# A retention-and-FFN kernel: k and q of two pairs loaded and transposed together, v behind them

## The chip, the cores and the metric

The kernel runs on one core of a Trainium2 chip. The metric is the device time of one launch in microseconds: 224.27 us is the median of 3 runs of the kernel before (224.18 to 224.47). The profile is of one execution with a span of 224.2 us; the granted TensorE clock is full speed (1.0) throughout.

## The reference

Two stages follow each other. The first is a decayed linear attention with a recurrent state, for 4 batches, 8 heads, 768 tokens and head size 64; the second is a gated feed-forward layer over all 3072 tokens, with 512 features and 1536 hidden columns.

```python
gamma = 1.0 - 2.0 ** (-5.0 - np.arange(H))
for t in range(S):
    state = gamma[None, :, None, None] * state + np.einsum('bhd,bhe->bhde', k[:, :, t], v[:, :, t])
    y[:, :, t] = scale * np.einsum('bhd,bhde->bhe', q[:, :, t], state)

x = y.transpose(0, 2, 1, 3).reshape(B * S, H * D)
gate = 1.0 / (1.0 + np.exp(-(x @ w_gate)))
out = (gate * (x @ w_val)) @ w_out
```

All inputs and the output are float32 in HBM; the kernel computes in bfloat16 with float32 sums.

## The kernel before, in words

**Tiles.** The 768 tokens are cut into six chunks t of 128. A chunk of all four batches (512 rows) is one unit of the feed-forward stage. The attention works on "pairs": pair i = 2t + h is chunk t of batches 2h and 2h + 1, all 8 heads. So there are twelve pairs; pairs 4 and 5 are chunk 2, pair 6 is the first half of chunk 3.

**Attention of a pair.** Its k, q and v are loaded by GpSimd with a cast to bfloat16: k and q in three DMAs each (`load_kq`, `load_swapped`, L62 to L74: one of 128 KB at L66 and two of 64 KB at L70), v in one of 256 KB (`load_v`, L57 to L60). For the scores, k and q are needed with the head dimension on the partitions. From pair 3 on this is done by two crossbar DMAs per pair, issued by SyncE (`xbar`, L216 to L220): one for k (`kqX<-kn`), one for q (`kqX<-qn`). Then:

- `quarter_scores` (matmuls of L248) needs the pair's transposed k and q
- `mask` (VectorE, L261) multiplies the scores by the decay
- `inter` (L271) multiplies transposed q by the state of the pair two before
- `intra` (L278) multiplies the masked scores by v
- `state` (L301) multiplies the scaled k (`scale_k`, GpSimd, L224) by v, and `state_sum` (L310) adds it to the state
- `y_out` (L294) writes the attention's result as the input of the feed-forward stage

`block(old, new, st)` (L316 to L336) puts these in the order that TensorE gets: inter of old, scores of new, intra of old, state of st.

**Feed-forward of a chunk.** `up` (twelve groups, matmuls of L391) computes gate and value; ScalarE takes the sigmoid (L419) and VectorE the product (L420). `down` (eight groups, L391 too) multiplies by w_out; ScalarE copies the sums out (L441) and SyncE stores them (L442). The feed-forward of chunk t runs while the attention of the next chunks is worked in between its groups.

**What sets the order.** Every engine executes its instructions in program order, and the order is written out by hand. After the first chunk, `plan` (L574 to L584) lists for every chunk t which step goes behind which of its 20 groups (0 to 11 are `up`, 12 to 19 are `down`). In the loop at L592 a step is emitted behind its group; but each step's instructions run as soon as their own engine comes to them. GpSimd has the loads, `scale_k` and `hold`, and is ahead of TensorE. SyncE has the crossbar DMAs and the output stores in one queue.

`hold` (L536 and L537) is a copy of one column of transposed data on GpSimd, whose result nobody uses. It makes GpSimd wait until that crossbar DMA has landed, so that the loads listed behind it don't run beside the transfer. By default it waits for q (`which=1`), with a second argument of 0 for k.

**Around the change.** Before the plan starts, L556 to L559 put on GpSimd `scale_k(3)`, `hold(3, 0)` and all loads of pairs 4 and 5 in the order k, q, v of 4, k, q, v of 5 (`load_next`, L530 to L532). In the plan for t = 1, `xbar(4)`, `scale_k` of 4 and 5, `hold(4)` and the loads of pair 6 stand behind group 4, and `xbar(5)` behind group 7. Pair 4's scores and its state stand behind group 11, pair 4's inter and intra with pair 5's scores and state behind group 14, and pair 5's inter and intra with pair 6's scores and state behind group 18. `xbar(6)`, `scale_k(6)`, `hold(6)` and the loads of pair 7 stand behind group 12.

GpSimd's loads use a set of eight completion semaphores in turn, so a load can't be issued before the one eight places earlier has landed. The buffers concerned are six for k and v each, four for q and four for the transposed pairs (`kqX`).

Of the kernel before, what the change touches and what calls it, by code (L numbers as in the profile page):

```python
# [9 lines left out]
BF16 = mybir.dt.bfloat16  # L10
# [5 lines left out]
def kernel(  # L16
# [16 lines left out]
    C = 128  # L33
    NT = S // C
    NP = H // 2
# [10 lines left out]
    at = ctx.enter_context(tc.tile_pool(name="at", bufs=2))  # L46
# [3 lines left out]
    kn, qn, ks, vs, kqT = {}, {}, {}, {}, {}  # L50
# [6 lines left out]
    def load_v(i):  # L57
        t, h = divmod(i, 2)
        vs[i] = ld.tile([C, 2 * H, D], BF16, tag="vs", name="vs", bufs=6)
        nc.gpsimd.dma_start(out=vs[i], in_=v[2 * h:2 * h + 2, :, t * C:(t + 1) * C, :].rearrange("b h s d -> s (b h) d"))  # L60

    def load_swapped(tiles, x, i, tag, bufs):  # L62
        t, h = divmod(i, 2)
        tiles[i] = ld.tile([C, 2 * H, D], BF16, tag=tag, name=tag, bufs=bufs)
        src = x[2 * h:2 * h + 2, :, t * C:(t + 1) * C, :].rearrange("b h s d -> b s h d")
        nc.gpsimd.dma_start(out=tiles[i][:, 0:H], in_=src[0])  # L66
        dst = tiles[i][:, H:2 * H].rearrange("s (p e) d -> s e p d", e=2)
        pairs = src[1].rearrange("s (p e) d -> s e p d", e=2)
        for e in range(2):
            nc.gpsimd.dma_start(out=dst[:, e], in_=pairs[:, 1 - e])  # L70

    def load_kq(i):
        load_swapped(kn, k, i, "kn", 6)
        load_swapped(qn, q, i, "qn", 4)  # L74
# [138 lines left out]
                nc.tensor.transpose(tp[:, which, p, :], heads(x, j, p), ident)  # L213
        nc.scalar.copy(kqT[i][:, :, j], tp)

    def xbar(i):  # L216
        kqT[i] = at.tile([128, 2, 2, NP, C], BF16, tag="kqX", name="kqX", bufs=4)
        for which, x in enumerate((kn[i], qn[i])):
            nc.sync.dma_start_transpose(out=kqT[i][:, which].rearrange("d j p s -> d (j p) s"),
                                        in_=x.rearrange("s h d -> s (h d)"))  # L220

    def scale_k(i):
        ks[i] = ld.tile([C, 2 * H, D], BF16, tag="ks", name="ks", bufs=3)
# [207 lines left out]
    def down(t, b, lo, hi, split=None):  # L431
        split = t > 0 if split is None else split
        if lo == 0:
            po[b] = bank([128, 512])
        o = po[b]
        for n1 in range(lo, hi):
            product(split, o, hT[t][:, n1, b * C:(b + 1) * C], wo[:, n1, :], start=(n1 == 0), stop=(n1 == NFF - 1))
        if hi < NFF:
            return
        ob = ffn.tile([128, D_MODEL], F32, tag="ob", name="ob", bufs=4)  # L440
        nc.scalar.copy(ob, o)  # L441
        nc.sync.dma_start(out=out[rows(t, b):rows(t, b) + C, :], in_=ob)  # L442
# [87 lines left out]
    def load_next(i):  # L530
        load_kq(i)
        load_v(i)  # L532
# [3 lines left out]
    def hold(i, which=1):  # L536
        nc.gpsimd.tensor_copy(held, kqT[i][:, which, 1, NP - 1, C - 1:C])  # L537
# [12 lines left out]
    for j in range(2):  # L550
        mask(2, j, 0)
        mask(2, j, 1)
    xbar(3)
    for b in range(3):
        down(0, b, 9, 12)
    scale_k(3)  # L556
    hold(3, 0)
    load_next(4)
    load_next(5)  # L559
    down(0, 3, 0, 6)  # L560
    new_y(2)
    inter(2)
# [2 lines left out]
    for j in range(2):  # L565
# [6 lines left out]


    plan = {  # L574
        1: [(2, block, None, 3), (4, block, 3, None, 3), (4, xbar, 4), (4, scale_k, 4), (4, scale_k, 5), (4, hold, 4),
            (4, load_next, 6), (5, casts, 3), (7, xbar, 5), (11, block, None, 4, 4), (12, xbar, 6), (12, scale_k, 6),
            (12, hold, 6), (12, load_next, 7), (14, block, 4, 5, 5), (18, block, 5, 6, 6)],
        2: [(0, xbar, 7), (0, scale_k, 7), (0, hold, 7), (0, load_next, 8), (4, casts, 4), (8, block, 6, 7, 7), (10, xbar, 8),
            (10, scale_k, 8), (10, hold, 8), (10, load_next, 9), (14, casts, 5), (17, block, 7, 8, 8)],
        3: [(2, xbar, 9), (2, scale_k, 9), (2, hold, 9), (2, load_next, 10), (4, casts, 6), (8, block, 8, 9, 9), (10, xbar, 10),  # L580
# [46 lines left out]
```

## Time and profile before

| what | value |
|---|---|
| time | 224.27 us (224.18 to 224.47) |
| TensorE busy | 215.9 us, 96% of the span |
| VectorE, ScalarE, GpSimd busy | 124.6, 70.6, 100.3 us |
| loads issued by GpSimd (queue q0) | 80960 packets, 13.90 MB, 83.8% of 16 engines' span |
| SyncE's transfers and stores (queue q1) | 23648 packets, 11.21 MB, 25.7% |
| crossbar DMA, median from issue to landing | k 6.8 us, q 4.0 us |
| load of one v, median from issue to landing | 7.3 us |
| GpSimd waiting in `hold` for transposed q | 34.6 us in 6 waits |

How to read it: the busy time of an engine is its share of the whole span, but only waits on the engine that sets the end cost anything. GpSimd's 34.6 us in `hold` are made on purpose. The chain of waits goes from the last instruction back to what released each one; the timeline shows one engine's instructions in order, with a wait in brackets behind the row that waited; the DMA issues give the time from the issue of a transfer to its landing.

### The profile page before, as it was taken

Reading aid. Unit: us, or ns where it says so; the run is one execution under the profiler, and the core shown is the slowest. Engines: PE = TensorE matmul, PEld = TensorE weight load, DVE = VectorE, ACT = ScalarE, POOL = GpSimd, SP = SyncE. Lnnn points to the kernel's source line nnn. Section 1 sums busy time; section 2 is a strip of 40 time slices with the busy share of each in tenths; the row PEclk is TensorE's granted clock in tenths of the full one; section 3 lists DMA queues with packets and bytes.
Section 4 is the critical chain, followed back from the end, with each engine's and each line's share of the span. In section 5 each row is a group of like instructions: output and inputs, shape, how many; then the busy total and the mean of one; then the engine's idle time right before and its main releaser. Section 6 shows DMA issues by size and latency. Waiting matters only on the chain.

```text
span 224.2 us, 6376 instructions
## 1 busy us (share of the span) xinstructions
PE 215.9 (96%) x2760; PEld 126.4 (56%) x2766; DVE 124.6 (56%) x252; ACT 70.6 (31%) x122; POOL 100.3 (45%) x120
## 2 busy tenths in 40 slices
PE   7789999999999997999999999999999999999994
PEld 2544444569999654556556556555555555555554
DVE  6784963194963874845925744935654922333301
ACT  4883333243233121332321332321433321333221
POOL 7999647859792935819276082550000000000000
PEclk9999999999999999999999999999999999999999
DMA  9999999999999999999979979897600012100022
GB/s 132 147 166 185 196 202 174 170 156 236 155 123 130 134 129 196 162 92 92 125 105 174 169 50 123 90 136 126 140 3 0 3 47 96 47 4 1 3 94 94
DMA packets 105820, 25.84 MB, mean 115 GB/s; under 512 B 94784, under 2 KB 102848, under 8 KB 105792
## 3 DMA queue, kind: packets, MB, share of 16 engines
q0 software_dynamic: 80960, 13.90, 83.8%
q1 hardware_dynamic: 23648, 11.21, 25.7%
q8 instruction: 21, 0.34, 0.7%
q10 hardware_dynamic: 1184, 0.33, 0.6%
q14 instruction: 7, 0.06, 0.1%
HBM read 28.31 MB, written 6.29 MB: 154 GB/s over the span
## 4 chain that ended last, share of the span: by engine, by line
PE 60%; DMA 25%; POOL 12%; issue 1%; DVE 0%; POOLq 0%; SPq 0%
PE ff L391 56%; DMA kqX<-qn 7%; DMA wo<-in_moe_w_out_dram 5%; DMA qn<-in_q_dram 4%; DMA kn<-in_k_dram 3%; DMA wv<-in_moe_w_val_dram 3%; DMA kqX<-kn 2%; PE ff L278 2%; POOL kn L70 2%; POOL vs L95 2%; POOL wg L82 2%; POOL wv L82 1%; POOL kn L95 1%; POOL kn L66 1%; POOL qn L95 1%; PE ff L248 1%
## 5 line engine op out<-in xcount | busy, mean ns | idle before, releaser
L420 DVE TENSOR_TENSOR hT<-gs,ff 128x512 bf16<-128x512 f32 x72 | 48.4, 686 | 50.3 <-PE ff L391 47.0
L391 PE MATMUL ff<-xT,wv 128*64 128x512 bf16 (+2 forms) x608 | 70.0, 345 | 0.1
L391 PE MATMUL ff<-xT,wg 128*64 128x512 bf16 (+2 forms) x606 | 69.8, 345 | 0.1
L419 ACT ACTIVATE gs<-ff 128x512 f32<-128x512 f32 x72 | 42.8, 597 | 83.2 <-PE ff L391 76.4
L391 PE MATMUL ff<-wo,hT 128*64 128x512 bf16 (+3 forms) x580 | 64.5, 361 | 0.1
L391 PEld LDWEIGHTS <-wv 128*64 128x64 bf16 (+1 forms) x608 | 35.4, 109 | 23.5
L391 PEld LDWEIGHTS <-hT 128*64 128x64 bf16 (+1 forms) x582 | 32.7, 109 | 27.1
L391 PEld LDWEIGHTS <-wg 128*64 128x64 bf16 (+1 forms) x608 | 34.9, 109 | 23.2 <-DVE xT L294 0.2
L261 DVE TENSOR_TENSOR st<-ff,maskk 128x256 bf16<-128x256 f32 (+2 forms) x76 | 35.1, 492 | 7.4 <-PE ff L248 6.4
L441 ACT COPY ob<-ff 128x512 f32<-128x512 f32 x23 | 13.5, 586 | 58.6 <-PE ff L391 58.4
L294 DVE TENSOR_TENSOR xT<-ff,taby 128x512 bf16<-128x512 f32 x20 | 12.9, 686 | 25.4 <-PE ff L278 25.4
L537 POOL COPY held<-kqX 128x1 bf16<-128x1 bf16 x7 | 1.5, 211 | 37.1 <-DMA kqX<-qn 34.6
L70 POOL DMA_DIRECT2D kn<-in_k_dram x20 | 15.1, 765 | 2.3 <-DMA kn<-in_k_dram 1.1
L70 POOL DMA_DIRECT2D qn<-in_q_dram x20 | 15.3, 790 | 1.0 <-DMA wv<-in_moe_w_val_dram 0.6
L224 POOL TENSOR_TENSOR ks<-kn,tabsk 128x1024 bf16<-128x1024 bf16 x8 | 15.6, 1956 | 0.0
L60 POOL DMA_DIRECT2D vs<-in_v_dram x10 | 12.0, 1204 | 1.1 <-DMA wo<-in_moe_w_out_dram 1.0
L66 POOL DMA_DIRECT2D kn<-in_k_dram x10 | 9.3, 926 | 2.3 <-issue 1.5
L66 POOL DMA_DIRECT2D qn<-in_q_dram x10 | 9.1, 913 | 0.8 <-DMA wv<-in_moe_w_val_dram 0.8
L314 DVE TENSOR_TENSOR zb<-za,tabz 128x512 bf16<-128x512 f32 x10 | 7.3, 734 | 0.0
L464 PE MATMUL ff<-zero 128*128 128x512 bf16 x14 | 5.6, 542 | 1.2 <-DVE zero L139 1.2
L82 POOL DMA_DIRECT2D wv<-in_moe_w_val_dram x8 | 6.7, 864 | 0.0
L82 POOL DMA_DIRECT2D wg<-in_moe_w_gate_dram x8 | 6.6, 853 | 0.0
(74 smaller groups left out, 114.4 us busy)
## 6 DMA issues: line engine op xcount, KB each, us to landing
out_dram<-ob SPq DMA_DIRECT2D x23, 256.0 KB, 2.7
vs<-in_v_dram POOLq DMA_DIRECT2D x10, 256.0 KB, 7.3
kn<-in_k_dram POOLq DMA_DIRECT2D x13, 128.0 KB, 4.8
qn<-in_q_dram POOLq DMA_DIRECT2D x13, 128.0 KB, 4.7
wo<-in_moe_w_out_dram POOLq DMA_DIRECT2D x4, 384.0 KB, 9.1
kn<-in_k_dram POOLq DMA_DIRECT2D x20, 64.0 KB, 3.7
qn<-in_q_dram POOLq DMA_DIRECT2D x20, 64.0 KB, 4.9
wg<-in_moe_w_gate_dram POOLq DMA_DIRECT2D x4, 256.0 KB, 7.5
```

What stands on the lines that cost most here:

```text
L60: nc.gpsimd.dma_start(out=vs[i], in_=v[2 * h:2 * h + 2, :, t * C:(t + 1) * C, :].rearrange("b h s d -> s (b h) d"))
L66: nc.gpsimd.dma_start(out=tiles[i][:, 0:H], in_=src[0])
L70: nc.gpsimd.dma_start(out=dst[:, e], in_=pairs[:, 1 - e])
L82: nc.gpsimd.dma_start(out=dst[:, kk, cols], in_=w.rearrange("(kk p) n -> p kk n", p=128)[:, kk, cols])
L95: eng.dma_start(out=dst, in_=x[b:b + n, :, 0:C, :].rearrange("b h s d -> s (b h) d"))
L224: nc.gpsimd.tensor_tensor(ks[i], kn[i], tabsk[:, i // 2].rearrange("s j h -> s (j h)").unsqueeze(2) .to_broadcast([C, 2 * H, D]), op=ALU.mult)
L261: nc.vector.tensor_tensor(st[i, j][to, :, n], sc[i, j][e][of, :, n], maskk[to, e ^ j, :, n], op=ALU.mult)
L294: nc.vector.tensor_tensor(xT[t][0][:, :, c:c + C], y[i, j], taby, op=ALU.mult)
L391: nc.tensor.matmul(o[c], w[:, c], x, **marks)
L419: nc.scalar.activation(g, ps[0], AX.Sigmoid)
L420: nc.vector.tensor_tensor(hT[t][:, n1s[0]:n1s[-1] + 1, lo:hi], g.rearrange("p (i n) -> p i n", n=n), ps[1].rearrange("p (i n) -> p i n", n ...
L441: nc.scalar.copy(ob, o)
```

## The change

The loads before the plan bring only k and q of pairs 4 and 5. Then the four crossbar transfers of both pairs are issued one after the other, in the order q of 5, k of 4, q of 4, k of 5. As SyncE keeps its order, the first of them waits for the load that comes last, and so all four start when all four loads have landed. `hold(5, 0)` makes GpSimd wait for the last of the four; behind it come v of 4, v of 5 and k and q of 6. v of pair 6 moves behind `hold(6)`, just ahead of the loads of pair 7. Later pairs keep their order. The aim is that loads and crossbar transfers are in flight apart from each other, and not together. The arithmetic is the same.

```diff
-    def xbar(i):
-        kqT[i] = at.tile([128, 2, 2, NP, C], BF16, tag="kqX", name="kqX", bufs=4)
-        for which, x in enumerate((kn[i], qn[i])):
+    def xbar(*pairs):
+
+        for i in pairs:
+            kqT[i] = at.tile([128, 2, 2, NP, C], BF16, tag="kqX", name="kqX", bufs=4)
+        order = [(i, which) for i in pairs for which in range(2)]
+        if len(pairs) > 1:
+            order = order[-1:] + order[:-1]
+        for i, which in order:
             nc.sync.dma_start_transpose(out=kqT[i][:, which].rearrange("d j p s -> d (j p) s"),
-                                        in_=x.rearrange("s h d -> s (h d)"))
+                                        in_=(kn[i], qn[i])[which].rearrange("s h d -> s (h d)"))
...
-    load_next(4)
-    load_next(5)
+    load_kq(4)
+    load_kq(5)
...
-        1: [(2, block, None, 3), (4, block, 3, None, 3), (4, xbar, 4), (4, scale_k, 4), (4, scale_k, 5), (4, hold, 4),
-            (4, load_next, 6), (5, casts, 3), (7, xbar, 5), (11, block, None, 4, 4), (12, xbar, 6), (12, scale_k, 6),
-            (12, hold, 6), (12, load_next, 7), (14, block, 4, 5, 5), (18, block, 5, 6, 6)],
+        1: [(2, block, None, 3), (4, block, 3, None, 3), (4, xbar, 4, 5), (4, scale_k, 4), (4, scale_k, 5), (4, hold, 5, 0),
+            (4, load_v, 4), (4, load_v, 5), (4, load_kq, 6), (5, casts, 3), (11, block, None, 4, 4), (12, xbar, 6), (12, scale_k, 6),
+            (12, hold, 6), (12, load_v, 6), (12, load_next, 7), (14, block, 4, 5, 5), (18, block, 5, 6, 6)],
```

## The prediction

> **What bounds the kernel now.** I read the page first: TensorE is busy for 215.9 of 224.2 us, so only its few idle stretches can be won and every new one is lost. Then the chain of waits in order of time (start, length, what):
>
> ```profile
> 76.48 3.42 DMA qn<-in_q_dram
> ...
> 80.02 5.98 DMA kqX<-qn
> 86.00 0.14 issue
> 86.13 0.57 PE ff L248 x19
> 86.71 0.58 PE ff L278 x16
> 87.28 0.25 PE ff L301 x16
> 87.54 16.84 PE ff L391 x156
> ```
>
> Up to 86.13 the chain runs over loads and crossbar transfers; from there on it is TensorE alone, line after line, to the end. So whatever moves the matmuls of pair 6 (at 86 to 87) moves the end by the same amount. The timeline of TensorE shows the places where it meets the data (start, length, line, what, count, idle time):
>
> ```profile
> 72.63 0.54 PE L248 MATMUL ff<-kqX 64*64 64x128 bf16 x32
> 73.11 0.44 PE L301 MATMUL ff<-vs,ks 128*64 128x64 bf16 x16
> ...
> 77.36 0.42 PE L271 MATMUL ff<-kqX,zb 64*64 64x128 bf16 x16
> 77.61 0.62 PE L248 MATMUL ff<-kqX 64*64 64x128 bf16 x32
> ...
> 84.16 0.42 PE L271 MATMUL ff<-kqX,zb 64*64 64x128 bf16 x16
> 86.13 0.58 PE L248 MATMUL ff<-kqX 64*64 64x128 bf16 x32 [1.56 <-DMA kqX<-qn]
> 86.65 0.64 PE L278 MATMUL ff<-st,vs 128*64 128x128 bf16 x16
> 87.12 0.42 PE L301 MATMUL ff<-vs,ks 128*64 128x64 bf16 x16
> ```
>
> The scores of pair 6 follow pair 5's L271, which takes 0.25 us to the next start (77.36 to 77.61 for pair 4), so they were due at 84.41 and began at 86.13: a stall of 1.72 us, the only one over half a microsecond after 20 us. That is the most that the change can win. Note also who needs v: state (L301) runs at 73.11 for pair 4 and at 87.12 for pair 6, right behind the scores. Third, the timeline of GpSimd, which issues all loads in program order:
>
> ```profile
> 58.92 1.58 POOL L70 DMA_DIRECT2D kn<-in_k_dram  x2 [1.14 <-DMA kn<-in_k_dram]
> ...
> 72.00 0.19 POOL L537 COPY held<-kqX 128x1 bf16<-128x1 bf16 x1 [4.11 <-DMA kqX<-qn]
> 72.45 0.94 POOL L66 DMA_DIRECT2D kn<-in_k_dram  x1 [0.26 <-issue]
> ...
> 77.21 1.23 POOL L60 DMA_DIRECT2D vs<-in_v_dram  x1
> ```
>
> The held copy at 72.00 is the gate: pair 6 is not asked for before pair 4's q has come through the crossbar. Last, the DMA issues (KB each, us to landing), in short windows at 62.9 us and at 158 us:
>
> ```profile
> vs<-in_v_dram POOLq DMA_DIRECT2D x1, 256.0 KB, 10.3
> kqX<-qn SPq DMA_TRANSPOSE x1, 10.4
> ```
> ```profile
> kqX<-kn SPq DMA_TRANSPOSE x1, 3.4
> kqX<-qn SPq DMA_TRANSPOSE x1, 3.3
> ```
>
> Beside a load a crossbar transfer and the load both take over 10 us; with no load in flight a transfer takes 3.3 to 3.4. This is what the change goes for.
>
> **What the Trainium skill says.** "DMA: Bandwidth & Descriptors", section "Issuing engines are not separate DMA queues": transfers of all issuers run on the same 16 engines and interleave. The 10.4 against 3.3 us agrees. Same page, "Anatomy of one DMA — SWDGE (gpsimd) path": one GpSimd load costs about 2.0 us plus its bytes by 436 GB/s; the trace shows more (a 128 KB part of k, whose float32 source is 256 KB, issued at 72.45, took 4.0 us; the price gives 2.6). "TensorE: Matmul & The Clock Gate", Part 1: after a whole idle window of about 3.4 us the clock falls to half for about as long. No stall of before is so long, and the granted clock is 1.00 in all windows of 10 us.
>
> **Part 1: k and q of 4 and 5 first.** Up to 55.76 nothing changes on GpSimd (k and q of pair 4). Then k of pair 5 takes the place of v of pair 4. The wait at 58.92 ends when the load eight places earlier has landed (the first part of k4, issued at 50.93, 7.7 us to landing by the DMA issues: 58.6). k4 and q4 are three loads each; with v4 as the seventh, the ninth was k5's second part. Without v4 it is k5's last part that waits there till 58.9. Then the three parts of q5 follow at the pace of the L70 and L66 rows (0.75 for k5's last, then 0.92 and 0.77): q5 starts at 59.65, 60.55 and 61.3. Its last part is issued at 61.3 in place of 62.1. In the quiet stretch of pair 6 that issue took 3.42 us to landing (first fence). No transfer runs beside it now, so q5 is there at 64.7 (bounds 64.0 and 65.8: some engines may lag behind the output stores). The two scale_k (1.95 us each) end at 66.0 on GpSimd and are hidden behind the transfers.
>
> **Part 2: four transfers in one go.** The first to be issued waits for q5, the last one to load; SyncE serves its queue in order, so pair 4's transfers, issued at 59.99 and 61.49 before, now wait for 64.7 too. An issue takes 1.24 us (median of L219); the last of the four starts 3 x 1.28 = 3.85 later, at 68.55, and lands 3.4 later by the quiet rows: 71.95. Lower bound 3.1 (fastest row), upper: 1 to 3 us more if a queue of four does not run at the quiet pace, as in the L219 issues of 1.8 to 3.1 us. Pair 4's own transfers are second and third, there by 70.7, before TensorE wants them at 72.6: hidden, and nothing won. hold(5, 0) waits for k of pair 5, the last of the four: 72.0, as good as the same moment as before.
>
> **Part 3: v of 4 and 5 behind that wait.** This is a new wait: behind the held copy GpSimd now has v4, v5 and then all loads of pair 6, and TensorE waits for v4. Issue 0.45 after the copy (72.00 to 72.45 before): 72.45. Landing of a lone v: no such row. Lower bound 3.2 (the skill's price, 2.0 + 512 KB / 436 GB/s). Upper 5.0: k of pair 6, as many rows in three issues, 72.45 to 77.5 (74.13 + 3.4). The three take 2.45 us to issue and one v 1.22, so 5.0 - 1.2 = 3.8 if nothing else limits; I take 4.1. v4 lands at 76.55; state of pair 4 was at 73.11: **TensorE stalls 3.4 us** (bounds 2.3 and 6). v5 lands in time for 77.6 + 3.4.
>
> **Part 4: pair 6.** k and q of pair 6 are issued two v issues (2.44 us) later: from 74.9. The last part of q6 starts 4.03 later (76.48 - 72.45), at 78.9. Landing 3.4 (pair 6 before) to 4.9 (pair 8, whose k transfer fell on its q load); the same happens here, and v4 and v5 lie ahead, so 4.0: 82.9. Its transfer, with no v beside it: 3.5 instead of 5.98, so 86.4 instead of 86.00. The undisturbed transfer gives back just what the two v issues took. TensorE, late by 3.4, wants it only at 87.8: **the 1.72 us stall is gone.**
>
> **Part 5: v of 6 behind hold(6).** Before, v6 was issued at 77.21 and landed 8.2 later at 85.4, in time. Now it goes out at 86.4 + 0.45 = 86.85, and lands 4.1 + 0.4 later (three output stores now run beside it): 91.35. State of pair 6 would be ready to start at 87.12 - 1.72 + 3.4 = 88.8: **a second stall of 2.5 us.** It starts at 91.35 in place of 87.12: +4.2. k of pair 7 follows at 88.1 in place of 86.6, 1.5 later, while TensorE is 4.2 later: no new wait. All after that moves as one.
>
> Sum: + 3.4 (v4) - 1.7 (pair 6's scores) + 2.5 (v6) = 4.2; 224.3 + 4.2 = **228.5**.
>
> **Rivals.** (a) v6 in time, only v4 late: + 3.4 - 1.72 = 1.7, 226.0. For it: a lone v nearer 3.2 and q6 at 3.4 draw v6 forward. Against it: v6 would have to be issued by 84.3 (88.8 - 4.5). (b) Four transfers in a row do not run at the quiet pace: each of the two rounds ends 1 to 1.5 later and so does v6: + 2 to 3, 231. For it: the L219 issues of 2 to 3 us; against it: those all fell on a busy load queue. (c) Faster: the quiet transfers end so early that both v are in time, and only the 1.72 is left: 222.5. That asks for v4 at 73.1, so hold(5, 0) open at 68.6, which is the time of the fourth issue: the profile speaks against it. A milder form, where each bound is at its best (64.0, 3.1, 3.7), still ends near + 0.5, 224.8. (d) The first stall of 3.4 us halves the clock for about as long: 1.7 us lost, but inside the wait for v6 (2.5), so 228.5 remains; in (a) it makes 227.7.
>
> **Numbers.** Main case 0.62, (a) with (d) 0.15, (b) 0.17, (c) 0.06. The main case with its bounds is 226.8 to 230.3; with most of (a) and (b) the range is 225.9 to 231.2. Faster 0.04, same 0.03, slower 0.93.
>
> **What would show it.** State of pair 4 (L301 behind the scores at 72.6) with 3 to 4 us of idle TensorE until vs landed; held near 72.0; v loads at 72.5 with a landing of 4; scores of pair 6 without a wait; state of pair 6 waiting 2 to 3 us for vs; from there the same pace to the end. I am wrong if q5 lands before 62, if four transfers take well under 7 us together, or if state gets its v without a wait.

## The result and the profile after

The changed kernel takes 233.18 us (231.77 to 237.09 in 6 runs) against 224.31 us before: 1.039 times as long, with a 95% interval of 1.033 to 1.045. The ratio leaves out the run of 237.09 us, which counts as a slow one. The forecast was 228.5 us with a range of 225.9 to 231.2. The direction was right; the loss was twice what was forecast, 8.9 us in place of 4.2.

The profiled execution took 232.13 us with a span of 230.3 us, 6.1 us more than the span shown of before. The chain of waits of the changed kernel, in order of time (start, length, what):

```profile
78.39 4.33 DMA qn<-in_q_dram
...
82.85 3.29 DMA kqX<-qn
...
86.27 0.19 POOL held L542
86.46 0.27 issue
86.72 6.35 DMA vs<-in_v_dram
93.08 0.14 issue
93.21 0.44 PE ff L306 x16
```

The crossbar transfer of q6 takes 3.29 us where it took 5.98 before: that part does what it is for. But behind the held copy there is now a load of v, which did not stand in the chain before, and the chain passes to TensorE only at 93.21 and not at 86.13 (L306 is the state, L301 before). The timeline of TensorE (L253 are the scores, L276 inter, L283 intra, L396 the feed-forward):

```profile
72.63 0.54 PE L253 MATMUL ff<-kqX 64*64 64x128 bf16 x32
76.93 0.64 PE L306 MATMUL ff<-vs,ks 128*64 128x64 bf16 x16 [3.75 <-DMA vs<-in_v_dram]
77.35 6.64 PE L396 MATMUL ff<-wo,hT 128*64 128x512 bf16 x36
83.92 0.42 PE L276 MATMUL ff<-kqX,zb 64*64 64x128 bf16 x16
...
90.96 0.52 PE L253 MATMUL ff<-kqX 64*64 64x128 bf16 x32
91.41 0.64 PE L283 MATMUL ff<-st,vs 128*64 128x128 bf16 x16
93.21 0.44 PE L306 MATMUL ff<-vs,ks 128*64 128x64 bf16 x16 [1.16 <-DMA vs<-in_v_dram]
```

Both states wait for v, the scores of pair 6 (90.96) wait for nothing. Between the two stalls stands something that the forecast had only as a rival (d): 36 feed-forward matmuls take 6.57 us to the next start (77.35 to 83.92) and 3.98 before. The stretches of 2 us tell why (length, busy times and counts of five engines, granted clock, DMA share, GB/s):

```profile
74.00:76.00 2.00, 0.00 (x0) 0.00 (x0) 1.93 (x5) 0.00 (x0) 2.00 (x3) 0.94 1.87 119
76.00:78.00 2.00, 1.07 (x20) 0.85 (x22) 1.50 (x3) 0.00 (x0) 2.00 (x4) 0.50 2.12 135
78.00:80.00 2.00, 2.00 (x12) 0.95 (x10) 0.30 (x1) 0.00 (x0) 1.20 (x2) 0.50 2.41 153
80.00:82.00 2.00, 2.00 (x12) 0.94 (x10) 0.00 (x0) 0.00 (x0) 0.51 (x1) 0.50 1.77 112
82.00:84.00 2.00, 2.00 (x20) 0.99 (x20) 0.00 (x0) 0.58 (x1) 1.39 (x1) 0.86 0.75 134
```

The clock falls to half during the stall and stays there for 6.8 us: the missing shares are 0.06 + 3 x 0.50 + 0.14 = 1.70, times 2 us, divided by the half that is missing. GpSimd's timeline shows the gates:

```profile
71.62 0.19 POOL L542 COPY held<-kqX 128x1 bf16<-128x1 bf16 x1 [7.20 <-DMA kqX<-kn]
72.09 2.37 POOL L60 DMA_DIRECT2D vs<-in_v_dram  x2 [0.28 <-issue]
...
86.27 0.19 POOL L542 COPY held<-kqX 128x1 bf16<-128x1 bf16 x1 [2.88 <-DMA kqX<-qn]
86.72 1.23 POOL L60 DMA_DIRECT2D vs<-in_v_dram  x1 [0.27 <-issue]
```

A gate is a held copy that has to wait for a transfer. The two open at 71.6 and 86.3, where the forecast had 72.0 and 86.4.

### The profile page after: what moved, and what is told of

Read it like the earlier page. It is cut to its first block, busy times and chain, and to the rows that moved or that the text cites. A ratio compares the mean times of both kernels' runs of the same rounds, so it can differ in the third digit from the quotient of the medians.

```text
span 230.3 us, 6373 instructions
## 1 busy us (share of the span) xinstructions
PE 218.1 (95%) x2760; PEld 129.6 (56%) x2766; DVE 125.5 (55%) x252; ACT 70.6 (31%) x122; POOL 99.9 (43%) x120
## 4 chain that ended last, share of the span: by engine, by line
PE 58%; DMA 19%; POOL 18%; SPq 2%; issue 1%; DVE 0%; POOLq 0%
PE ff L396 55%; DMA wo<-in_moe_w_out_dram 5%; DMA qn<-in_q_dram 3%; DMA kqX<-kn 3%; DMA kn<-in_k_dram 3%; DMA vs<-in_v_dram 3%; POOL wg L82 3%; POOL wv L82 3%; POOL kn L70 2%; SPq L224 2%; POOL kn L66 2%; POOL vs L60 2%; POOL vs L95 2%; PE ff L283 1%; DMA kqX<-qn 1%
## 5 line engine op out<-in xcount | busy, mean ns | idle before, releaser
L396 PE MATMUL ff<-xT,wv 128*64 128x512 bf16 (+2 forms) x608 | 70.2, 345 | 0.1
L396 PE MATMUL ff<-xT,wg 128*64 128x512 bf16 (+2 forms) x606 | 70.0, 345 | 0.1
L396 PE MATMUL ff<-wo,hT 128*64 128x512 bf16 (+3 forms) x580 | 67.1, 372 | 0.1
L396 PEld LDWEIGHTS <-hT 128*64 128x64 bf16 (+1 forms) x582 | 34.1, 112 | 28.3 <-issue 2.6
L396 PEld LDWEIGHTS <-wv 128*64 128x64 bf16 (+1 forms) x608 | 36.3, 109 | 22.6
L396 PEld LDWEIGHTS <-wg 128*64 128x64 bf16 (+1 forms) x608 | 35.8, 109 | 22.3 <-DVE xT L299 0.2
L446 ACT COPY ob<-ff 128x512 f32<-128x512 f32 x23 | 13.5, 585 | 64.7 <-PE ff L396 64.6
L299 DVE TENSOR_TENSOR xT<-ff,taby 128x512 bf16<-128x512 f32 x20 | 12.9, 686 | 29.7 <-PE ff L283 29.7
L306 PE MATMUL ff<-vs,ks 128*64 128x64 bf16 x128 | 3.6, 202 | 4.9 <-DMA vs<-in_v_dram 4.9
L319 DVE TENSOR_TENSOR zb<-za,tabz 128x512 bf16<-128x512 f32 x10 | 8.0, 808 | 0.0
```

The costliest lines, as they stand in the source:

```text
L299: nc.vector.tensor_tensor(xT[t][0][:, :, c:c + C], y[i, j], taby, op=ALU.mult)
L319: nc.vector.tensor_tensor(zb[i], za[i], tabz[:, i // 2 + 1].unsqueeze(3).to_broadcast([128, 2, NP, D]), op=ALU.mult)
L396: nc.tensor.matmul(o[c], w[:, c], x, **marks)
```

## The experiments

The theory: v of 4 and v of 6 come a whole landing after their gate opens, at the very place where TensorE wants them; the chain of gates up to v of 6 sets the end, the first stall is hidden under the second, and a clock halved behind an idle TensorE adds to it. Rivals: the first late v alone is the cost; loads and transfers as such slow the kernel down; the output stores delay v of 6. All ratios are to runs of the kernel before on the same chip.

| label | what it is | median us (runs) | ratio (95% interval) |
|---|---|---|---|
| after_again | the changed kernel | 234.16 (4) | 1.046 (1.039 to 1.054) |
| e1_fill | stall before state of 4 filled | 236.46 (4) | 1.053 (1.051 to 1.055) |
| e2_states_late | all three states moved later | 229.28 (4) | 1.020 (1.013 to 1.027) |
| e3_state45_late | states of 4 and 5 later, not of 6 | 234.18 (4) | 1.041 (1.034 to 1.047) |
| e4_state6_late | state of 6 later alone | 231.11 (4) | 1.028 (1.024 to 1.031) |
| e9_fill_both | both stalls filled | 233.90 (4) | 1.040 (1.034 to 1.047) |
| e10_fill_stores_later | the same, no stores beside v6 | 235.27 (4) | 1.045 (1.037 to 1.053) |
| e11_v6_ahead | only v of 6 back ahead | 230.95 (4) | 1.027 (1.021 to 1.032) |
| e7_one_go | one go alone, v of 4, 5, 6 early | 227.60 (4) | 1.011 (1.007 to 1.015) |
| e5_v6_behind | only v of 6 behind, rest as before | 231.16 (4) | 1.026 (1.021 to 1.031) |
| e6_v6_behind_state_late | the same, state of 6 later | 224.66 (20) | 0.9996 (0.9979 to 1.0013) |

**The changed kernel and the kernel before once more.** No edit.

> The changed kernel, unaltered, beside the next three on one chip. Theory A (the two late v set the time, the halved clock behind the first stall delays the output stores and so the second v): state of pair 4 waits 3.5 to 4 us for vs, the clock is half for about 6.8 us behind it, state of pair 6 starts about 6 us later than in the kernel before; ratio 1.03 to 1.045. Theory B (the spread between 231.8 and 237 comes from the clock): runs above 234 show a lower mean clock than those at 232.

> The kernel before once more, for its profile. The profiled execution of before took 225.99 us where its median is 224.27; the forecast took its 1.72 us stall at pair 6 for a fixed cost. Theory A: in a usual execution (224.0 to 224.4) the scores of pair 6 start within 0.5 us of 84.4 and the span is 222.5, so there was hardly anything to win. Rival: the stall is there in every execution, and the profiled one was slow somewhere else.

The kernel before had 224.59 us and a span of 222.8. Its TensorE timeline at pair 6:

```profile
84.56 0.42 PE L271 MATMUL ff<-kqX,zb 64*64 64x128 bf16 x16
84.81 0.52 PE L248 MATMUL ff<-kqX 64*64 64x128 bf16 x32
85.26 0.64 PE L278 MATMUL ff<-st,vs 128*64 128x128 bf16 x16
85.73 0.42 PE L301 MATMUL ff<-vs,ks 128*64 128x64 bf16 x16
```

The scores follow inter after 0.25 us: no stall. So the 1.72 us stall, which the forecast took for what could be won, belongs to the profiled execution of before, which took 225.99 us where the median is 224.27. In this usual execution TensorE has no idle stretch there, and nothing was to be won; e6 below bears that out over 20 runs.

The changed kernel's profiled execution this time took 237.47 us. Both waits for v are long:

```profile
77.54 0.52 PE L306 MATMUL ff<-vs,ks 128*64 128x64 bf16 x16 [4.10 <-DMA vs<-in_v_dram]
...
95.68 0.64 PE L306 MATMUL ff<-vs,ks 128*64 128x64 bf16 x16 [4.08 <-DMA vs<-in_v_dram]
```

The clock was half behind both, 3.4 and 6.8 us long, and its mean was 0.976. The other three runs took 234.1 to 234.2 us with a mean clock of 0.985; the first three runs of the result, at 232, had 0.983 to 0.985. So the mean clock marks the slowest executions, but does not part 232 from 234. Where in the program the half clock lies matters too, as the next experiment shows.

**e1_fill**

```diff
-(11, block, None, 4, 4)
+(11, block, None, 4), (11, keep_on, 17), (11, block, None, None, 4)
```

> Changed kernel with 17 matmuls of 512 zero columns (17 x 0.216 = 3.7 us) put between scores and state of pair 4, so that TensorE is busy while it waits for vs; they are work on top that nobody uses. Theory A: the clock stays at 1.00, TensorE reaches pair 6 about 2.8 us earlier, the stores go out earlier, v of pair 6 lands in 4.5 to 5.5 us instead of 6.4, and the end is 1 to 2 us earlier than the changed kernel's: +4.2 to +5.2 over the kernel before. Rival (the loss of the clock goes into the end in full): 2.8 us earlier than the changed kernel, +3.4. Rival (v6 lands when it does, the clock costs nothing): same as the changed kernel.

The edit puts 17 matmuls on zeros, whose result nobody uses, between the scores and the state of pair 4. A miss, and an instructive one: 236.5 us, no faster than the changed kernel. Three of the four runs of that beside it took 234.1 to 234.2 and one 237.5, so the intervals of the two ratios overlap. TensorE's timeline and two stretches:

```profile
77.34 0.44 PE L306 MATMUL ff<-vs,ks 128*64 128x64 bf16 x16
...
94.47 0.64 PE L306 MATMUL ff<-vs,ks 128*64 128x64 bf16 x16 [4.74 <-DMA vs<-in_v_dram]
```
```profile
76.00:80.00 4.00, 4.00 (x47) 1.99 (x47) 2.22 (x4) 0.00 (x0) 3.78 (x5) 1.00 2.05 131
...
94.00:96.00 2.00, 1.53 (x22) 1.06 (x24) 1.16 (x3) 0.00 (x0) 1.22 (x2) 0.50 1.92 122
```

The filler keeps the clock up behind state of 4. TensorE then comes to state of 6 earlier, has to wait 4.74 us in place of the 1.16 of the changed kernel's first profile, and the clock falls there. Behind the first stall the half clock only used up time in which TensorE would have waited for v of 6 anyway; behind the second nothing hides it. From this state to the next inter it is 19.24 us (94.47 to 113.71) against 17.21 in the changed kernel's first profile (93.21 to 110.42), 2.03 more. Another 1.26 comes from v of 6 landing later (94.47 against 93.21): its gate opened at 87.6 and not at 86.3, which is not shown to be the filler's doing. The last 0.9 lies behind the last inter and was not traced further.

**e9_fill_both** has the filler of e1_fill and this:

```diff
-(18, block, 5, 6, 6)
+(18, block, 5, 6), (18, keep_on, 14), (18, block, None, None, 6)
```

> Changed kernel with both stalls filled with matmuls on zero columns that nobody uses, 17 ahead of state of 4 (3.7 us) and 14 ahead of state of 6 (3.0 us). Theory A: the clock stays at 1.00 throughout; v of 6 lands at 93 to 94.5 beside the output stores and sets the end: about 8 to 9 us after the 85.4 of an execution without stalls, less the halved clock of e1_fill (2.1 us): 232 to 234. Rival (the clock falls for another reason than idle time): still a mean of 0.985.

As expected: clock 1.00 in the profiled execution, 233.9 us.

```profile
94.66 0.44 PE L306 MATMUL ff<-vs,ks 128*64 128x64 bf16 x16 [1.18 <-DMA vs<-in_v_dram]
```

State of 6 starts 8.93 us behind the 85.73 of the usual execution of before, and the last 144 feed-forward matmuls start at 218.18 against 209.22, 8.96 later. So with a full clock the time up to v of 6 alone carries the whole loss.

**e3_state45_late**

```diff
-(11, block, None, 4, 4) ... (14, block, 4, 5, 5), (18, block, 5, 6, 6)
+(11, block, None, 4) ... (14, block, 4, 5, 4), (18, block, None, None, 5), (18, block, 5, 6, 6)
```

> Changed kernel with state of 4 moved from group 11 to 14 and of 5 from 14 to 18; state of 6 stays where it is. So TensorE does not wait for v of 4 any more, only for v of 6. Theory A (the chain of loads and transfers up to v of 6 sets the time, the first stall is hidden under the second): state of 6 starts at 93 to 95 as in the changed kernel, TensorE waits for it 4 us or more and the clock is halved behind it; time as the changed kernel's or slower, 232 to 237. Rival (v of 4 is the main cost): 228 or less.

234.2 us: as slow as the changed kernel, although nothing waits for v of 4. The rival that the first late v alone is the cost has fallen. Two other waits show instead:

```profile
87.53 0.86 PE L253 MATMUL ff<-kqX 64*64 64x128 bf16 x32 [2.72 <-DMA kqX<-qn]
...
93.11 0.64 PE L306 MATMUL ff<-vs,ks 128*64 128x64 bf16 x16 [3.73 <-DMA vs<-in_v_dram]
```

The scores of pair 6 wait for transposed q and the state of 6 for v. It starts at 93.11, as in the changed kernel's first profile (93.21).

**e4_state6_late**

```diff
-(18, block, 5, 6, 6)]
+(18, block, 5, 6)]
-(4, casts, 4)
+(3, block, None, None, 6), (4, casts, 4)
```

> Changed kernel with only the state of pair 6 moved, to group 3 of the next chunk. Theory A: v of 4 is late as before, so +3.8 for that stall, +2.8 for the halved clock, -1.7 for the scores of pair 6 that no longer wait: +4.9 over the kernel before, about 1.2 us faster than the changed kernel. Rival (v of 6 sets the end alone): +2 or less.

231.1 us, 6.8 more than before.

```profile
77.33 0.64 PE L306 MATMUL ff<-vs,ks 128*64 128x64 bf16 x16 [3.15 <-DMA vs<-in_v_dram]
77.74 6.62 PE L396 MATMUL ff<-wo,hT 128*64 128x512 bf16 x36
84.29 0.42 PE L276 MATMUL ff<-kqX,zb 64*64 64x128 bf16 x16
```

The stall of 3.15 us on v of 4 and the half clock (36 matmuls in 6.55 us) now go into the end in full. The expected +4.9 subtracted 1.72 us for pair 6, which a usual execution doesn't have: 4.9 + 1.7 = 6.6.

**e2_states_late** moves all three: state of 4 to 14, of 5 to 18, of 6 to group 3 of the next chunk, as in the two before.

> Changed kernel with the three states, which are the first users of v, each moved to a later place: state of 4 from behind group 11 to 14, of 5 from 14 to 18, of 6 from 18 to group 3 of the next chunk. Loads and transfers are untouched. Theory A: no stall on vs any more, clock 1.00, scores of pair 6 wait 1.7 us for the transposed q as in the kernel before (86.1 against 84.4): within 0.5 us of the kernel before. Rival (loads and transfers in themselves slow TensorE or the engines down): still 3 us or more slower than before.

A miss: 229.3 us, 2.0% slower than before, though no state waits any more. The timeline:

```profile
84.47 0.42 PE L276 MATMUL ff<-kqX,zb 64*64 64x128 bf16 x16
87.40 0.86 PE L253 MATMUL ff<-kqX 64*64 64x128 bf16 x32 [2.51 <-DMA kqX<-qn]
```

The scores of pair 6 start 2.7 us late, and the clock falls there too (0.85, 0.50 and 0.80 in the stretches from 86 to 92). Two things put k and q of 6 back: they are issued behind v of 4 and 5, and the gate ahead of these opens at 72.66, where it opened at 70.06 in the usual execution of before (and at 70.0 to 70.8 in the profiles of e6 and e5, which leave pairs 4 and 5 as before). The undisturbed transfer of q of 6 (3.0 us) does not make up for both. In the changed kernel this lies under the first stall.

**e11_v6_ahead** takes back the last part of the change; **e5_v6_behind** does it alone, on the kernel before.

```diff
 e11: the changed kernel with
-(4, load_kq, 6) ... (12, hold, 6), (12, load_v, 6), (12, load_next, 7)
+(4, load_next, 6) ... (12, hold, 6), (12, load_next, 7)
 e5: the kernel before with
-(4, load_next, 6) ... (12, hold, 6), (12, load_next, 7)
+(4, load_kq, 6) ... (12, hold, 6), (12, load_v, 6), (12, load_next, 7)
```

> Changed kernel with v of 6 back ahead of its transfers. Theory A: v of 4 is late as in the changed kernel, +3.8 to +4.2 with a halved clock behind it (+1.7 to +2.8); v6 is in time, transposed q of 6 lands later (88 to 90) but TensorE comes only at 90: +5.5 to +7 in all, 230 to 231.5. Rival (v6 behind its transfers saves more than it costs): as slow as the changed kernel, 233 or more.

> The kernel before with the last part of the change alone: v of pair 6 behind hold(6), pairs 4 and 5 as before. Theory A (a load put behind a transfer costs a whole landing where its first user stands close): transposed q of 6 lands undisturbed at about 82.5, v6 is issued at 83 and lands 5 to 6 later, at 88 to 89; state of 6 stands at 85.7, so +2.5 to +3.5, and where the clock falls behind it another 1 to 2: 227 to 229. Rival (v6's lateness comes only from the first part): within 0.5 of before.

e11 is at 231.0 as expected: one go with v of 4 and 5 late costs 2.7%, and state of 6 no longer waits. e5 is at 231.2, above the 227 to 229 expected. TensorE's timelines, e11 first:

```profile
79.65 0.64 PE L306 MATMUL ff<-vs,ks 128*64 128x64 bf16 x16 [5.12 <-DMA vs<-in_v_dram]
```
```profile
90.57 0.64 PE L301 MATMUL ff<-vs,ks 128*64 128x64 bf16 x16 [3.87 <-DMA vs<-in_v_dram]
```

The 5.12 us are of an execution of 232.46 us, above e11's median of 230.95, so its usual stall may be shorter. In e5 the gate opened later than assumed (v6 was issued at 84.8, transposed q of 6 still took 4.7 us) and the clock was half for 6.8 us behind the stall. Each part of the change costs about 2.6% alone, both together 3.9 to 4.6%: less than the sum, as the first stall is hidden under the second.

**e6_v6_behind_state_late** is e5 with state of 6 in group 3 of the next chunk, as in e4.

> As e5_v6_behind, and state of 6 moved to group 3 of the next chunk, where v6 has long landed. Theory A: no wait on v6; as a usual execution of before has no stall at pair 6 either, the same time as before within 0.3 us, perhaps without its slower executions (225 and above). Rival (the 1.72 us stall of the profiled run is usual): 222.6.

0.9996 (0.9979 to 1.0013): the late v costs nothing once its first user stands later, and nothing is won either. The rival that the 1.72 us stall is usual, which asked for 222.6 us, has fallen.

**e7_one_go**

```diff
-    load_kq(4)
-    load_kq(5)
+    load_next(4)
+    load_next(5)
-(4, load_v, 4), (4, load_v, 5), (4, load_kq, 6) ... (12, load_v, 6), (12, load_next, 7)
+(4, load_next, 6) ... (12, load_next, 7)
```

> The first part without late v: loads of 4 and 5 in the old order with both v ahead of the transfers, then the four transfers in one go, hold(5, 0), then k, q, v of 6 as before. Theory A: the transfers start behind q5 at about 65 and run beside v5, the last lands at 73 to 75, pair 6 is asked for 1 to 3 us later than before and its scores wait 1 to 4 us: 226 to 230. Rival (the transfers in one go are the gain, v the loss): 224 or less.

227.6 us. Even with every v early, four transfers in one go lose 1.1%. GpSimd's and TensorE's timelines:

```profile
74.95 0.19 POOL L542 COPY held<-kqX 128x1 bf16<-128x1 bf16 x1 [8.00 <-DMA kqX<-kn]
```
```profile
87.42 0.54 PE L253 MATMUL ff<-kqX 64*64 64x128 bf16 x32 [2.59 <-DMA kqX<-qn]
```

The gate is the last of four transfers and not the second: it opens at 74.95 in place of 70.06 in the usual execution of before (72.00 in the first profile), and pair 6 comes late.

**e10_fill_stores_later and two more: why v of 6 takes longer than v of 4.** v of 6 took 6.4 us to land in the changed kernel, v of 4 took 4.7. e10 is e9_fill_both with 8 filler matmuls at the second place, with eight buffers for ob in place of four and this:

```diff
+        if t == 1 and b < 3:
+            stored.append((b, ob))
+            return
         nc.sync.dma_start(out=out[rows(t, b):rows(t, b) + C, :], in_=ob)
...
+(19, store_all)
```

> As e9_fill_both, with 8 matmuls ahead of state of 6, and with the first three output stores of chunk 1 put off to group 19, so that no store runs beside v of 6. Theory A (stores make v of 6 late): v of 6 lands 4.5 to 4.8 us after its issue, as the lone v of 4 did, instead of 5.5 to 6.8, and the time is 1 to 2 us below e9_fill_both. Rival (the stores are not the cause): the landing still takes 5.5 us or more and the time is the same.

A miss: no store runs beside it, and v of 6 still takes 6.1 us. So a late landing needs no store. e12 is e10 with this function called between load_v(6) and load_next(7), so that GpSimd spends time there; e13 is e10 again:

```diff
+    def spend(i):
+        for _ in range(2):
+            nc.gpsimd.tensor_tensor(pad, kn[i], ...)
```

> As e10_fill_stores_later (both stalls filled, no store beside v of 6), and GpSimd spends two multiplications of 1.95 us each, whose result nobody uses, between the issue of v6 and the loads of pair 7. So v6 is alone in the load queue. Theory C (the loads queued behind v6 share the engines with it and draw its landing out): v6 lands 4.0 to 4.9 us after its issue, state of 6 starts 1.2 us or more earlier. Rival (what stands behind it does not matter): 5.5 to 6.3 us again.

> e10_fill_stores_later once more, for a second look at the landing of v6 with the loads of pair 7 behind it and no store beside it. Theory C: again 5.5 to 6.3 us. Rival (6.1 was an accident of one execution, such as the instruction fetch that lay beside it): below 5.2 us.

e12 had 233.6 us (2 runs, 1.039 with an interval of 1.032 to 1.046), e13 234.1 (2 runs, 1.041, 1.035 to 1.047). v of 6 took 5.8 us in e12 with nothing else in the load queue, and 5.6 in e13. So a late landing needs no loads behind it either. What is left in e12 shows in its DMA issues at 88.3 us, in its queues from 91.5 to 92.6, and in its stretches of half a microsecond:

```profile
vs<-in_v_dram POOLq DMA_DIRECT2D x1, 256.0 KB, 5.8
```
```profile
q8 instruction: 1, 0.02, 5.3%
```
```profile
91.50:92.00 0.50, 0.50 (x4) 0.26 (x3) 0.50 (x2) 0.00 (x0) 0.50 (x1) 1.00 2.42 180
...
92.50:93.00 0.50, 0.01 (x1) 0.00 (x0) 0.50 (x2) 0.00 (x0) 0.50 (x1) 1.00 0.57 27
93.00:93.50 0.50, 0.00 (x0) 0.00 (x0) 0.47 (x2) 0.00 (x0) 0.50 (x2) 1.00 0.25 10
```

Most of v is there by 92.6; then the rate falls from 180 to 10 GB/s, about the share of one of 16 engines (180 / 16 = 11), and this rest takes another microsecond. Beside v lies one instruction fetch of 16 KB, which in a window of 1.1 us takes 5.3% of 16 engines' time: 0.93 us of one engine. By the Trainium skill, "DMA: Bandwidth & Descriptors", section "Why a DMA increments its semaphore by 16 and not by 1", all 16 engines must report before a load counts as landed, so an engine held up for a microsecond holds up the load. Such a fetch lies beside the packets of v of 6 in after_again, e1, e5, e6, e9, e10 and e13 as well, with landings of 5.6 to 6.8 us. In e3 (5.0 us) it ends as v's first packets move, and in e4 (5.4 us) there is none. That fits, but the fetch was not moved on its own, so it isn't shown; and it can't be the only cause, as the 6.4 us of the changed kernel had no fetch beside them.

There the start was late. The first packet of v of 6 moved 2.8 us after its issue in the changed kernel, 2.7 in after_again and 2.4 in e4, but after 1.9 to 2.1 in the other profiles in which v of 6 stands behind its gate, and after 1.9 for v of 4. In just these three an output store was issued 0.6 to 0.9 us behind v, and its packets ran first: from 88.65 to 89.45 us only the store's queue moved anything in the changed kernel. So about 0.9 of the 1.7 us by which v of 6 took longer than v of 4 lies beside a store, ahead of v's first packet. The rest stays open.

## Why the prediction was right and wrong

The mechanism was forecast: two late v, the second deciding, no wait for the scores of pair 6. Two terms of the sum were wrong. Part 5 gave v of 6 a landing of 4.5 us, and it took 6.4. The step "the 1.72 us stall is gone" subtracted a stall that a usual execution doesn't have. A third was put at nothing: a loss of clock behind the second stall, which cost 2.9 us in the one slower execution that was profiled.

**The gates: right, by two errors that cancel at the first.** q5 was there at 63.2 (59.80 issued, 3.40 to landing; forecast 64.7), as GpSimd did not have to wait at k5's last part (till 58.9 in the forecast): k4 had landed sooner. But from then to the last of the four transfers it took 8.3 us (63.2 to 71.5) where the forecast had 7.25: the last was issued 5.0 us after the first (63.35 to 68.35) and not 3.85. The first gate opened at 71.6 (72.0), v of 4 landed 4.7 us after its issue (4.1) at 76.8 (76.55), state of 4 stalled 3.8 us (3.4). q6 was there at 82.7 (82.9), its transfer took 3.3 us (3.5), v of 6 was issued at 86.72 (86.85). At that issue the forecast was off by 0.1 us. That the first gate stands "as good as the same moment as before" holds only for the execution of 225.99 us; in the usual one it opened at 70.06, so with four transfers in one go it stood 1.6 us later.

**Part 5, the landing of v of 6: too small.** The forecast had 4.1 + 0.4 = 4.5 us; it was 6.4 in this execution and 5.0 to 6.8 in the others. That is 1.9 of the 4.7 us by which the median missed. The lone v was too small by 0.6, as v of 4 shows; for what runs beside it the forecast added 0.4, a guess without a row, where v of 6 took 1.7 longer than v of 4. Some of the 1.9 would have been lost without it: TensorE, slowed by the half clock, could not have started the state of 6 before 91.9 (91.41 and the 0.47 that the row before takes to its next start), 0.5 behind the forecast's 91.35.

**What is won: nothing.** The sum took 1.72 us off for pair 6 and added the rest to the median of 224.27. But the stall was part of an execution of 225.99, and the median has none. One must not take a stall from a slow execution and subtract it from the median: in the usual execution state of 6 starts at 85.73, or 85.33 if the scores of pair 4 are laid on each other (73.03 there, 72.63 here); the forecast's own 91.35 less that is +6.0, and 224.3 + 6.0 is 230.3. So this step is 1.7 us of the miss.

**The clock: half right.** Rival (d) let the first stall halve the clock and hide it under the wait for v of 6. That is what the first profile shows, but with a clock that is half for 6.8 us and not for about 3.4, and a loss of 2.74 us and not 1.7. Against the usual execution of before, from scores of pair 4 to state of pair 6 it is 20.58 us in place of 12.70 (73.03 to 85.73), 7.88 more: 3.82 for v of 4, 2.74 for the half clock (0.15 in the state, 2.59 in the 36 matmuls), 1.33 for v of 6. But the forecast gave no clock loss to the second stall. Where that is long, as in the execution of 237.47 us, it does: 4.17 for v of 4, 1.67 for the clock behind it, 4.25 for v of 6, and then 2.92 behind state of 6 (to the next inter 20.10 us against 17.18), 13.0 together; the spans differ by 12.9. The Trainium skill ("TensorE: Matmul & The Clock Gate", Part 1) has the fall after an idle window of about 3.4 us. The stretches at half clock agree with windows of that length: they are 3.4, 6.8 or 10.2 us long. It is 3.4 where TensorE worked from the start of the stretch (e2, and the first in after_again), 6.8 where the stretch began inside a wait (the changed kernel, e1, e4, e5, e11), and 10.2 in e3, where a second wait lies in it: cut into pieces of 3.4 us from its start, each stretch ends with the first piece in which TensorE worked throughout. The idle time needed does not agree: a wait of 2.51 us in e2 was enough, while one of 2.59 in e7 was not. In e4 the clock was half from 76.1, 1.9 us after the scores ended at 74.2. So it is no safe rule that a stall under 3.4 us leaves the clock alone.

Together: 228.5 + 1.9 (landing) + 1.7 (no stall to win) = 232.1, the level of the first three runs, 231.8 to 232.4. The one profile of a slower execution, at 237.47, lies higher by a later v of 6 and by the clock behind it; what puts the usual runs at 234 was not profiled and stays open.

**Rival (b)**, four transfers not at the quiet pace, came true by 1.1 us of the 2 to 3 it had: they were issued more slowly, though the last landed 3.15 us after its issue. Q5's early landing took it back. **Rival (c)**, faster, did not come true. Rival (a), v of 6 in time, is what e11 makes by hand, and it is at 231.0, above the 226.0 to 227.7 given. The same 1.7 us is part of that; the stall of 5.1 us in place of 3.4 is another as far as its profile goes, which is of a slower execution than its median.

## What to carry to other kernels

A load that is put behind a gate to keep it away from a transfer is as late as the gate plus a whole landing: look for its first user, and either leave the load ahead or move the user, as e6 does at no cost. Before a stall in a profile is counted as a gain, check that the profiled execution's time is the median's. And when TensorE stalls for some microseconds (here from 2.5 us on, though not each time), allow for a clock loss behind the last of the stalls, since only what lies ahead of a later wait is hidden.

## What was not expected of the hardware

- Filling an idle TensorE with matmuls that nobody uses kept the clock at 1.00 behind the first stall, but did not make the kernel faster (236.5 against 234.2 us on the same chip): the half clock moved from a place where it was hidden to one where it was not.
- A wait of 2.51 us was enough to halve the clock for 3.4 us, and one of 2.59 us in e7 was not. Where the half clock began inside a wait it lasted 6.8 or 10.2 us and not 3.4, though TensorE worked again for most of it (76.93 to 82.57 in the changed kernel).
- An output store issued 0.6 to 0.9 us behind a load of v moved its packets first, and v's first packet came 0.4 to 0.9 us later than in the other profiles.
- The last microsecond of a load of 256 KB can run at 10 GB/s, about the share of one DMA engine; an instruction fetch of 0.93 us on one engine lay ahead of it.
